# Keys transposed on VectorE and moved with the queries, under one written order for all engines

## The chip, the cores and the metric

The kernel runs on one core of a Trainium2 chip. The metric is the device time of one execution in microseconds, the median of the runs. A profiled execution gives the span from the first to the last instruction and a record of each instruction.

## The reference

Two blocks follow each other. A gated linear recurrence with a complex gate runs over 768 steps for 4 x 8 sequences of width 48, and its result is the input of a feed-forward block with 3072 tokens, 384 features and 2048 hidden units. All data are float32; the weights arrive as float64.

```python
mag = sqrt(a_re**2 + a_im**2)
a = (a_re + 1j*a_im) * minimum(mag, 0.999) / (mag + 1e-6)
for t in range(768):                       # per batch b of 4 and head h of 8
    S = a[t][:, None] * S + outer(k[t], v[t])
    y[t] = q[t] @ real(S)
x = y, heads side by side                   # (3072, 384)
h = x @ w_in                                # (3072, 2048)
g = h * erf(softplus(h))
out = g @ w_out                             # (3072, 384)
```

## The kernel before

`quotient_path` does the work; `product_path` is a general fallback behind a branch that tests the range of the data, and these inputs do not enter it. The tokens are cut into NU = 12 units of 256, each of C = 2 chunks of 128 tokens. Three units make one of the four sequences in time.

The recurrence is written as attention with decay. The gate's magnitude and angle are summed over time by matmuls against triangular matrices (`g_decay` or `g_total`, `g_angle`: tiles `sum`), and ScalarE makes exponentials (`pr`) and sines and cosines (`CS`) of the sums. VectorE multiplies q and k by them (`prep`: `qr`, `qt`, `kr`, `kt`), which gives rows of 96 numbers per head, the real and the imaginary half side by side. For the scores both must lie with the 96 on partitions. Scores are then masked (`A`), and `xT` adds A times v and the query times the carried state S (tiles `y`), 32 columns at a time in four column groups of TensorE. `state` makes the next S from k and v (tile `kv`).

How q and k come into columns is what the change touches:

- In unit 0, `cols` transposes q and k by TensorE (against `ident`, tile `tr`, L1009), and a copy brings them to `Q` and `kT` (L1018).
- From unit 1 on, q goes another way: `turn` lets VectorE transpose blocks of 32 x 32 (`X`, L1025), and 12 DMAs a chunk on SyncE's queue (SP) move the blocks to their partitions (`Q`, L1030). `Q` and `X` have one buffer each. k still goes through `cols`: 8 transposes on TensorE and two copies on ScalarE a chunk.

The feed-forward part works by units too: `ff_in` (tile `hps`, L1109, then a copy to `h`), `softplus` (four passes of ScalarE over 128 x 2048), `erf_times_h` (a Gelu on ScalarE and four passes of VectorE), and `ff_out_8` or `ff_out_7` (tiles `ops`, L1169 and L1207), the latter with seven products in place of eight by sums of blocks. The weights come as 64-bit words and are narrowed to float32 in 16 pieces by `narrow` (tiles `raw`, `word`, L790 to L806), and are read a second time (`again`) to be looked through. `w_in_sb` is laid out as 128 x 3 x 2048, so a piece of 256 hidden units is three runs in each partition.

The order of the work is set by a plan: each step has a due time in units (`WHEN`), the steps are sorted by it and issued in that order,

```python
    for _, f in sorted(plan, key=lambda e: e[0]):
        f()
```

and a scheduler then arranges the instructions of each engine. For the first steps, and for ScalarE where its function tables change, the order is kept as issued (`InOrder`, `in_order`). `warm` issues matmuls whose result is not read.

Of the kernel before, what the change touches and what calls it, by code (L numbers as in the profile page):

```python
# [35 lines left out]
def weave(*streams):  # L36
# [5 lines left out]
    for _, _, _, step in sorted(order, key=lambda e: e[:3]):  # L42
# [4 lines left out]
WHEN = {'a00': [0.2503, 0.7795, 0.1335, 0.1031, -0.5748, 0.1112, 0.3413, 0.3135, 0.2977, 0.4533],  # L47
 'a01': [0.4583, -0.1745, 0.4592, 0.4654, 0.4351, 0.5509, 0.5645, 0.5706, 0.5738, 0.6413],
 'n': [0.9645, 0.7895, 0.7814, 0.9723, 0.9993, 1.2454, 1.3547, 1.3732, 1.6259, 1.9835, 1.9666, 2.0634, 2.0911, 2.6653, 2.517],
 'g1': [0.7386, 0.7506, 0.7936, 0.8248, 0.8347, 0.8715, 0.878],  # L50
 'att': {1: [[0.9545, 1.3618], 1.0648], 2: [[1.7319, 2.0993], 0.8095], 3: [[3.0299, 3.594], 1.0991]},
 'gate': {2: [1.2001, 1.3019, 1.3116, 1.4094, 1.3878, 1.4777, 1.3631],
          3: [1.4851, 1.5487, 1.7904, 1.9989, 2.1384, 2.0754, 2.128],
          4: [2.4992, 2.6362, 2.8477, 3.2431, 3.3368, 3.699, 2.4826]},
 'hps': {0: [[0.7464, 0.847], [1.0328, 1.4318]],
         1: [[1.783, 2.003], [2.3859, 2.68]],
         2: [[2.8628, 3.209], [3.3359, 3.9229]],
         11: [[12.1478, 12.1509], [12.3502, 12.7439]]},
 'act': {0: [1.8595, 2.395],
         1: [3.3067, 3.698],  # L60
         2: [4.1613, 4.4383],
         3: [4.9661, 5.2089],
         4: [5.7479, 6.0159],
         10: [12.0452, 12.2596],
         11: [12.5676, 13.0911]},
 'ops': {0: [3.4509, 3.4886, 3.7821],
         1: [3.4648, 4.4529, 4.6258],
         2: [4.5583, 4.8264, 5.0683],
         3: [5.5746, 5.649, 6.1029],
         10: [11.9993, 12.5968, 12.9211],  # L70
         11: [13.0067, 13.2826, 13.5712]},
 'T': 5.3262,
 'gr': [-1.4884, -1.4376, -1.1567, -0.9311, -0.6027, -0.494, -1.1755],
 'st': [-0.0295, 0.1798, 0.1707, 0.2187, 0.2039, 0.2378, 0.3865],
 'lead': {0: -0.1195, (1, 0): -0.0719},
 'turn': [0.0319, 0.043],
 'lq': -0.6408,
 'hr': [1.1054, 1.4916, 1.607, 1.9359],
 'ar': [1.4604, 1.9924],
 'or': [2.1463, 2.6719, 3.1818],  # L80
 'c1': 0.4351,
 'er': 0.201,
 'ag': [5.3391, 6.7346, 7.1057, 8.2917, 8.8347, 10.8654, 10.6123],
 'n1': 2,
 'rest': 11.7803,
 'ok': 13.7659,
 'al': [[11.1278, 12.8576], [11.9156, 12.5677]],
 'c1g': [0.7517, 0.7897, 0.4817],
 'warm': 0.025}


WARM = (20, 0, 16, 2, 10, 6)

class InOrder:


    def __init__(self, tc, engine):
        self.tc, self.engine, self.on = tc, engine, False

    def __getattr__(self, name):  # L100
        emit = getattr(self.engine, name)
        if not self.on:
            return emit
        return lambda *args, **kw: self.tc.keep_in_program_order(emit(*args, **kw))
# [510 lines left out]

@with_exitstack
def quotient_path(
# [20 lines left out]
    vector, scalar = InOrder(tc, nc.vector), InOrder(tc, nc.scalar)  # L638
# [44 lines left out]
    cold = zp.tile([P, P], FP, tag="z", name="cold")  # L683
    vector.memset(cold, 0.0)
# [12 lines left out]
    w_in_sb = const.tile([P, KD, FF], FP, name="w_in_sb")  # L697
# [19 lines left out]
    order = mybir.DependencyInfo(mybir.DependencyClass.NoSync, mybir.DependencyReason.DATA)  # L717

    def act(func, **kw):
        sets = [nm for nm, fs in TABLES.items() if func in fs]  # L720
        if not sets:
            ins = scalar.activation(func=func, **kw)
            if T.get("kept"):
                in_order(ins)
            return
        if T.get("table") != sets[0]:
            T["table"] = sets[0]
            in_order(scalar.preload_act_table_set(sets[0]))  # L728
        in_order(scalar.activation(func=func, **kw))  # L729

    def in_order(ins):
        if "act" in T:
            tc.add_manual_dep(ins.ins, T["act"].ins.name, order, reason="table order")
        T["act"] = ins
# [5 lines left out]


    def load(pool, names, sources, u, engines, cc=(0, C)):
        for nm in names:
            if cc[0] == 0:
                T[nm, u] = pool.tile([P, C, H, D], FP, tag=nm, name=nm)
        for c in range(*cc):
            for nm, src, engine in zip(names, sources, engines):
                engine.dma_start(out=T[nm, u][:, c], in_=rows(src, u, c))

    def load_gates(u):  # L750
        if u < NU:
            load(lda, ("ar", "ai"), (a_re, a_im), u, (nc.sync, nc.sync if u > 0 else nc.scalar))

    def load_qkv(u, cc=(0, C)):
        if 0 <= u < NU:
            load(ldq, ("k", "q"), (k, q), u, (nc.sync, nc.sync), cc)
            t = T["v", u] = vbuf[u % 2]
            for c in range(*cc):
                for e in range(2):
                    src = rows(v, u, c).rearrange("t (h e) d -> e t h d", e=2)[e]  # L760
                    nc.sync.dma_start(out=side(t[:, c], e), in_=src)
# [6 lines left out]
    def narrow(i, dst, src, home):  # L768

        k_, n = dst.shape[1:]

        def seek(words, i):
            hi = words.bitcast(FP).rearrange("p (n w) -> p n w", w=2)[:, :, 1]
            vector.tensor_reduce(out=zeros[:, i:i + 1], in_=hi, axis=mybir.AxisListType.X, op=OP.min,  # L777
                                    apply_absolute_value=True)

        split = lambda t: t.rearrange("p (k n) -> p k n", k=k_)  # L780

        def get():
            T["raw", i] = home[0].tile([P, N], I64, tag=home[1], name="raw")
            nc.sync.dma_start(out=split(T["raw", i]), in_=src)

        def high():
            words = T["raw", i].bitcast(U32).rearrange("p (k n w) -> p k n w", k=k_, w=2)
            lo, hi = words[..., 0], words[..., 1]
            a = split(sp.tile([P, PARTS], U32, tag="S", name="word")[:, 0:N])
            ins = vector.tensor_scalar(out=a, in0=hi, scalar1=0x07FFFFFF, scalar2=3, op0=OP.bitwise_and,  # L790
                                       op1=OP.logical_shift_left)
            if "hold" in T:
                tc.add_manual_dep(ins.ins, T["hold"].ins.name, order, reason="place among others")
            vector.scalar_tensor_tensor(out=a, in0=hi, scalar=0xC0000000, in1=a, op0=OP.bitwise_and,
                                        op1=OP.bitwise_or)
            T["parts", i] = a, lo

        def low():
            _, lo = T["parts", i]
            ins = scalar.mul(out=lo, in_=lo, mul=2.0**-29)  # L800
            if i < 3:
                in_order(ins)

        def join():
            a, lo = T["parts", i]
            vector.tensor_tensor(out=dst.bitcast(U32), in0=a, in1=lo, op=OP.add)  # L806

        def use():
            high()
            low()  # L810
            join()

        def again():
            pool, tag = ((zp, "z"), (yp, "yy"))[i % 2]
            T["raw", i] = pool.tile([P, N], I64, tag=tag, name="again")
            nc.sync.dma_start(out=split(T["raw", i]), in_=src)

        def look():
            seek(T["raw", i], i)

        if i < 14:
            return get, use, again, look, high, low, join

        def again():
            for j, tag in enumerate(("ar", "ai")):
                T["raw", i, j] = lda.tile([P, n], I64, tag=tag, name="again")
                nc.sync.dma_start(out=T["raw", i, j], in_=src[:, j])

        def look():
            for j in range(2):  # L830
                seek(T["raw", i, j], 2 * i - 14 + j)

        return get, use, again, look, high, low, join

    def weights():

        none = lambda: None
        homes = [(rawp, "raw")] * 2 + [(hp, "h0")] * 2 + [(hp, "h1")] * 2 + [(rawp, "raw")] * 10
        steps = []
        for j in range(8):  # L840
            piece = (slice(None), slice(None), slice(j * 2 * P, (j + 1) * 2 * P))
            steps.append((w_in_sb[piece], w_in.rearrange("(i p) f -> p i f", p=P)[piece]))
# [16 lines left out]
    def sums_of_weights(r0, n):  # L859


        if r0 == 0:
            T["T1"], T["T2"] = [rawp.tile([P, 10, HD], FP, tag="raw", name=nm) for nm in ("T1", "T2")]
# [120 lines left out]
    def chunk(u, c):  # L984
# [17 lines left out]
        def cols(nm, g):  # L1002
            def f():
                if (nm, g) == ("q", 0):
                    columns()
# [440 lines left out]
```

## Time and profile before

| | |
|---|---|
| median of 3 runs | 716.7 us (714.72 to 717.21) |
| the profiled execution's own time | 716.54 us |
| its span | 714.8 us |
| TensorE busy | 685.7 us |
| VectorE busy | 575.5 us |
| ScalarE busy | 588.9 us |
| mean granted clock of TensorE | 0.987 |
| DMA packets on SP's queue | 166536, 61.88 MB |

In the profile PE is TensorE's matmuls, PEld its weight loads (which lie beside matmuls), DVE is VectorE, ACT ScalarE, SP SyncE, whose queue issues nearly all DMAs. Busy time is the union of an engine's instructions. In a row of a group, the two numbers after the bar are the busy time of the group in us and the mean of one instruction in ns; matmuls overlap, so their mean is longer than the distance from one to the next. An f32 matmul appears as two records, an f32 transpose as one. The last column is the idle time of the engine just before the group, and what ended it.

### The profile page before, as it was taken

The numbers are of one execution on the slowest core, as the hardware profiler recorded it, in microseconds if no ns is written. First come the engines' busy times: TensorE is split into PE (matmuls) and PEld (weight loads), VectorE is DVE, ScalarE is ACT, GpSimd is POOL, SyncE is SP. The second block draws the span as 40 slices with busy tenths as digits, with TensorE's granted clock in tenths as the row PEclk, the third lists the DMA queues.
The fourth block names the chain that finished last, engine by engine and source line by source line (L and its number), as shares of the span: only waits on it lengthen the run. The fifth ranks groups of instructions, "written<-read, shape, count | busy, mean of one in ns | idle before, by whom it ended". The sixth has DMA issues, their size and how long they took to land.

```text
span 714.8 us, 12640 instructions
## 1 busy us (share of the span) xinstructions
PE 685.7 (96%) x4872; PEld 584.1 (82%) x4872; DVE 575.5 (81%) x987; ACT 588.9 (82%) x763; POOL 1.1 (0%) x8
## 2 busy tenths in 40 slices
PE   9898898999999999999999999999999999999995
PEld 8777676776786767898998898898888898899984
DVE  6759889997686869999897989788998885977562
ACT  7777799999899978799997799798898864777660
POOL 0000000000000000000000000000000000000000
PEclk9889999999999999999999999999999999999998
DMA  9872866572222212434135433435225115000000
GB/s 205 234 177 54 185 155 154 142 121 48 64 52 66 45 45 43 135 69 90 23 81 152 123 64 82 123 68 164 36 56 134 24 39 183 24 1 11 12 24 28
DMA packets 168686, 63.18 MB, mean 88 GB/s; under 512 B 146836, under 2 KB 158376, under 8 KB 168616
## 3 DMA queue, kind: packets, MB, share of 16 engines
q1 hardware_dynamic: 166536, 61.88, 36.5%
q8 instruction: 40, 0.66, 0.4%
q10 hardware_dynamic: 2080, 0.39, 0.4%
q14 instruction: 30, 0.25, 0.1%
HBM read 48.82 MB, written 4.75 MB: 75 GB/s over the span
## 4 chain that ended last, share of the span: by engine, by line
PE 39%; ACT 30%; DVE 17%; DMA 7%; issue 3%; SPq 2%; DVEq 0%; ACTq 0%
PE hps L1109 14%; PE ops L1207 8%; ACT L728 7%; ACT yy L729 6%; ACT z L729 5%; PE ops L1169 4%; PE sc L1039 3%; PE y L1087 3%; DVE yy L1138 3%; DVE z L1137 3%; DVE e L1139 2%; ACT e L729 2%; DVE h L1140 2%; SPq L1030 2%; DMA again<-in_moe_w_out_dram 2%
## 5 line engine op out<-in xcount | busy, mean ns | idle before, releaser
L1109 PE MATMUL hps<-xT,w_in_sb 128*128 128x256 f32 x1152 | 270.5, 383 | 4.3 <-DVE w_in_sb L806 3.3
L1109 PEld LDWEIGHTS hps<-xT,w_in_sb 128*128 128x128 f32 x1152 | 215.0, 191 | 41.0 <-DVE w_in_sb L806 4.7
L728 ACT ACT_TABLE_LOAD x94 | 120.6, 1283 | 1.5
L1137 DVE TENSOR_TENSOR z<-z,yy 128x512 f32<-128x512 f32 x96 | 63.0, 684 | 32.3 <-ACT e L729 31.6
L729 ACT ACTIVATE e<-z 128x512 f32<-128x512 f32 x96 | 57.3, 627 | 30.8 <-DVE h L1140 30.4
L1111 ACT COPY h<-hps 128x512 f32<-128x512 f32 x96 | 55.0, 575 | 32.8 <-PE hps L1109 32.7
L1169 PE MATMUL ops<-w_out_sb,h 128*128 128x384 f32 x224 | 77.9, 490 | 0.6 <-DVE h L1140 0.5
L1207 PE MATMUL ops<-w_out_sb,h 128*128 128x192 f32 x384 | 71.7, 328 | 0.2 <-DVE o L1218 0.2
L1207 PEld LDWEIGHTS ops<-w_out_sb,h 128*128 128x128 f32 x384 | 63.9, 190 | 3.8 <-issue 1.0
L1138 DVE SCALAR_TENSOR_TENSOR yy<-z,yy 128x512 f32<-128x512 f32 x96 | 62.9, 682 | 0.4
L1139 DVE TENSOR_TENSOR e<-e,yy 128x512 f32<-128x512 f32 x96 | 62.9, 682 | 0.3
L1140 DVE SCALAR_TENSOR_TENSOR h<-e,h 128x512 f32<-128x512 f32 x96 | 63.0, 681 | 0.2
L1169 PEld LDWEIGHTS ops<-w_out_sb,h 128*128 128x128 f32 x224 | 41.4, 190 | 25.8 <-DVE o L1177 1.2
L1039 PE MATMUL sc<-Q,kT 96*128 96x128 f32 x384 | 50.7, 284 | 6.7 <-DMA Q<-X 2.6
L729 ACT ACTIVATE z<-h 128x2048 f32<-128x2048 f32 x24 | 45.9, 1914 | 13.1 <-DVE seen L777 10.1
L1039 PEld LDWEIGHTS sc<-Q,kT 96*128 96x128 f32 x384 | 48.0, 197 | 10.7 <-ACT kT L1018 4.4
L1207 PE MATMUL ops<-T,S 128*128 128x192 f32 x256 | 46.8, 327 | 0.1
L729 ACT ACTIVATE z<-z 128x2048 f32<-128x2048 f32 x24 | 45.9, 1911 | 0.3
L729 ACT ACTIVATE yy<-yy 128x2048 f32<-128x2048 f32 x24 | 45.9, 1913 | 0.3
L729 ACT ACTIVATE yy<-z 128x2048 f32<-128x2048 f32 x24 | 45.9, 1912 | 0.2
L1042 DVE TENSOR_TENSOR A<-sc,triu 128x512 f32<-128x512 f32 x48 | 32.5, 683 | 14.9 <-PE sc L1039 14.8
L1207 PEld LDWEIGHTS ops<-T,S 128*128 128x128 f32 x256 | 42.6, 190 | 1.8 <-DVE S L1221 0.7
(128 smaller groups left out, 996.2 us busy)
## 6 DMA issues: line engine op xcount, KB each, us to landing
Q<-X SPq DMA_DIRECT2D x264, 32.0 KB
raw<-in_moe_w_in_dram SPq DMA_DIRECT2D x8, 768.0 KB
raw<-in_moe_w_out_dram SPq DMA_DIRECT2D x8, 768.0 KB
again<-in_moe_w_in_dram SPq DMA_DIRECT2D x8, 768.0 KB
ar<-in_a_re_dram SPq DMA_DIRECT2D x24, 192.0 KB
k<-in_k_dram SPq DMA_DIRECT2D x24, 192.0 KB
q<-in_q_dram SPq DMA_DIRECT2D x24, 192.0 KB
v<-in_v_dram SPq DMA_DIRECT2D x48, 96.0 KB
```

The lines of the kernel that those rows point to most:

```text
L728: in_order(scalar.preload_act_table_set(sets[0]))
L729: in_order(scalar.activation(func=func, **kw))
L1039: nc.tensor.matmul(out=ps[:, j, :], lhsT=head("k", g * HG + j), rhs=head("q", g * HG + j), start=True, stop=True)
L1042: vector.tensor_tensor(out=A, in0=ps, in1=triu.unsqueeze(1).to_broadcast([P, HG, P]), op=OP.mult)
L1109: nc.tensor.matmul(out=ps[:, e, :], lhsT=w_in_sb[:, kd, f0:f0 + P], rhs=T["xT", u][:, kd, :], start=(kd == 0), stop=(kd == KD - 1))
L1111: scalar.copy(out=T["h", u, sl][:, i:i + 2, :], in_=ps)
L1137: vector.tensor_tensor(out=z, in0=z, in1=y, op=OP.mult)
L1138: vector.scalar_tensor_tensor(out=y, in0=z, scalar=-2.0, in1=y, op0=OP.add, op1=OP.mult)
L1139: vector.tensor_tensor(out=e, in0=e, in1=y, op=OP.mult)
L1140: vector.scalar_tensor_tensor(out=h, in0=e, scalar=1.0 / RT2, in1=h, op0=OP.add, op1=OP.mult)
L1169: nc.tensor.matmul(out=ps, lhsT=lhsT, rhs=w_out_sb[:, i, :], start=i == HALF, stop=i == KF - 1)
L1207: ins = nc.tensor.matmul(out=ps, lhsT=a(sl)[:, i], rhs=b(sl, i), start=sl == 0 and i == 0, stop=sl == NSL - 1 and i == HALF - 1)
```

## The change

1. From unit 1 on, keys go the way of the queries. `prep` lets VectorE transpose `kt` as well as `qt` into one tile `X` of twice the size, and `move` carries both at once: 12 DMAs a chunk as before, into one tile `KQ` of 16 heads (8 of k, 8 of q). Each head's 128 columns lie together in `KQ`, and a DMA fills 32 of them in each head. `X` and `KQ` have one buffer each. TensorE's transposes and the copies of `kT` remain in unit 0 alone.
2. Each step is a generator that stops where the engine changes, and one list, `ORDER`, names which step goes on next; a name appears once for each part of the step. The instructions of all engines stand in this order and no scheduler moves them. `WHEN`, `InOrder` and the manual dependencies are gone.
3. `w_in_sb` is laid out as 128 x 8 x 3 x 256, so that a piece is one run in each partition.
4. In `result` (before: `xT`) the products with A and with the state alternate as A, state, state, A instead of A, state, A, state. The warm-up matmuls read `ident`, and their number and places are in the list.

The diff, cut to its core:

```diff
-    w_in_sb = const.tile([P, KD, FF], FP, name="w_in_sb")
+    w_in_sb = const.tile([P, FF // (2 * P), KD, 2 * P], FP, name="w_in_sb")
...
-        def turn():
-            x = att1.tile([P, D2 // QUAD, H, QUAD], FP, tag="X", name="X")
-            src = st["q"].rearrange("p h u d -> p h (u d)").rearrange("p h (b d) -> p b h d", d=QUAD)
-            vector.transpose(out=x, in_=src)
-            columns()
-            for i in range(P // QUAD):
-                at = slice(i * QUAD, (i + 1) * QUAD)
-                for b in range(D2 // QUAD):
-                    nc.sync.dma_start(out=st["Q"][b * QUAD:(b + 1) * QUAD, i], in_=x[at, b])
...
+    def prep(nm, u, c):
...
+        if u > 0:
+            x = whole(att1, "X", (u, c), [P, D2 // QUAD, 2 * H, QUAD])
+            src = t.rearrange("p h u d -> p h (u d)").rearrange("p h (b d) -> p b h d", d=QUAD)
+            i = "kq".index(nm) * H
+            vector.transpose(out=x[:, :, i:i + H], in_=src)
+            yield
+
+    def columns(u, c):
+        return whole(att2, "KQ", (u, c), [P, 2 * H, P], bufs=1)
+
+    def move(u, c):
+        kq, x = columns(u, c), T["X", (u, c)]
+        for i in range(P // QUAD):
+            at = slice(i * QUAD, (i + 1) * QUAD)
+            for b in range(D2 // QUAD):
+                nc.sync.dma_start(out=kq[b * QUAD:(b + 1) * QUAD, :, at], in_=x[at, b])
+            yield
...
-    plan += [(WHEN["rest"], restore), (WHEN["ok"], check)]
-    for _, f in sorted(plan, key=lambda e: e[0]):
-        f()
+    with tc.manual_schedule():
+        for nm in ORDER.split():
+            if nm[0] == "u":
+                steps[nm] = warm(int(nm[1:].split("_")[0]))
+            next(steps[nm])
```

The list begins and goes on like this (`M` is a chunk's move, `A` scores and mask, `Y` the result, `K` and `Q` the preparation, `h`, `x`, `e`, `O` the feed-forward steps; the numbers are unit, chunk or slab, and part):

```python
ORDER = """
g0.0 u8_0 u2_40 u2_24 u4_38 u2_41 g0.0 u8_1 u2_39 u4_20 u2_25 u4_21 u2_34 g0.1 g0.1 t0.0 t0.0 o0.0 m0.0 m0.0
...
O2.14 e3.0.4 b4 h3.1.4 h3.1.4 h3.1.2 h3.1.2 x3.1 x3.1 x3.1 M5.0 M5.0 g7.0 M5.0 M5.0 a6.1 p6.0 p6.0 b0 S5.0 a6.1
```

## The prediction

> **What bounds the kernel now.** I read the first part of the page first (who is busy), then the groups by line (what the change touches), the waits of TensorE (PE), the windows by stage, and last a piece of the chain of waits.
>
> ```profile
> span 714.8 us, 12640 instructions
> PE 685.7 (96%) x4872; PEld 584.1 (82%) x4872; DVE 575.5 (81%) x987; ACT 588.9 (82%) x763; POOL 1.1 (0%) x8
> ```
>
> PE is busy 96% of the span; VectorE (DVE) and ScalarE (ACT) have a fifth to spare as a mean. The groups by line (count, then busy us and mean ns of one):
>
> ```profile
> L1009 PE MATMUL tr<-ident,kt 128*96 128x128 f32 x192 | 25.3, 273 | 2.6 <-DVE kt L995 2.3
> L1018 ACT COPY kT<-tr 96x512 f32<-96x512 f32 x46 | 25.3, 576 | 3.4 <-PE tr L1009 3.4
> L1025 DVE STREAM_TRANSPOSE X<-qt 128x768 f32<-128x768 f32 x22 | 21.3, 967 | 0.0
> ```
>
> The first two rows are what goes, the third is what comes a second time. Then who PE waited for (us in total, times, longest):
>
> ```profile
> PE hps L1109 <- DVE w_in_sb L806: 3.3, 3, 2.4
> PE sc L1039 <- DMA Q<-X: 2.6, 3, 1.0
> ...
> PE tr L1009 <- DVE kt L995: 2.3, 2, 2.0
> PE sc L1039 <- ACT kT L1018: 2.1, 3, 1.3
> ```
>
> All of PE's idle time is only 714.8 - 685.7 = 29.1 us, in many small pieces. By stage (windows; busy us of each engine, then the granted clock, the DMA engines' share and GB/s):
>
> ```profile
> 0.00:54.00 54.00, 49.72 (x359) 42.84 (x360) 35.55 (x72) 39.62 (x80) 1.08 (x8) 0.91 0.90 205
> 54.00:126.00 72.00, 63.77 (x516) 51.05 (x515) 63.73 (x101) 61.65 (x87) 0.00 (x0) 0.98 0.56 135
> 126.00:324.00 198.00, 195.70 (x1274) 151.75 (x1274) 165.24 (x276) 181.09 (x224) 0.00 (x0) 1.00 0.36 77
> 324.00:632.00 308.00, 301.29 (x2281) 271.12 (x2280) 261.48 (x449) 262.07 (x327) 0.00 (x0) 1.00 0.34 84
> ```
>
> From 126 to 632 us PE is the bound (98 to 99%), and from there to 702 us it is never idle. In 54 to 126 DVE is as full as PE (89%), ACT just behind; in 126 to 324 ACT is at 91%. Last the chain, from one result (y) to the next scores (sc):
>
> ```profile
> 606.85 2.59 PE hps L1109 x12
> 609.44 1.94 PE y L1087 x64
> ...
> 617.65 0.59 SPq L1030
> ...
> 618.29 1.83 DMA Q<-X
> ...
> 620.36 2.02 PE sc L1039 x16
> 622.39 1.30 PE ops L1207 x8
> ```
>
> It gives PE's paces: hps 2.59/12 = 0.216 us a record (an f32 matmul is two records, a transpose one), 192-wide ops 0.163, sc 0.112 within its group, y 0.030; in the same way 384-wide ops 0.323, kv 0.083, sums 0.323, tr 0.109 (in the timeline eight begin at 323.17 and the next group at 324.05). Every group's count times its pace is 657 us. So of 714.8 us, 58 are loss: up to the end of the y at 128.1 us 98.8 us of work are done (29 lost: start, half clock near 35 us), up to the y that ends at 634.2 it is 584 (21 more), then 0 until 707, and 7.8 for the last stores and the check.
>
> **The change part by part.**
>
> *K's transposes leave PE.* 22 chunks (all but the two of unit 0) x 8 = 176 of the 192: at the pace of 0.109 us 19.2 us, at the row's union (25.3/192 = 0.132) 23.2. Inside a row of matmuls the pace counts, so I take 19.2. This is on the bound.
>
> *ACT:* 44 copies of kT x 0.576 = 25.3 us go; in the new order of instructions ACT loads 3 tables more (100 for 97) x 1.283 (the mean of that row) = 3.8 come. Net -21.5, beside PE's work.
>
> *DVE:* 22 transposes more x 0.967 = 21.3 us (575.5 to 597). Beside PE where DVE has room; not in 54 to 126, where it is at 89%. Units 1 to 3 are prepared by about 150 us: 6 x 0.97 = 5.8 us fall there, and in the same stretch 6 x 8 x 0.109 = 5.2 us of PE's saving. I count 3 us of it as not realised.
>
> *The moves.* As many as before (12 a chunk, 264 on SP's queue), each 64 KB instead of 32, and the destination's runs fall from 1 KB to 32 elements of 4 bytes = 128 B: 512 packets for 32. Issue on SP is 0.59 us for a Q move, 0.5 to 0.6 for the loads of q, k and v with 512 to 1024 packets, so SP's issue costs the same; what the page does not show is the price of a 128 B packet. Bounds from the trace's windows:
>
> ```profile
> 315.00:318.00 3.00, 3.00 (x21) 3.00 (x20) 1.25 (x3) 2.97 (x6) 0.00 (x0) 1.00 0.16 39
> 324.00:327.00 3.00, 3.00 (x20) 2.74 (x19) 3.00 (x6) 2.99 (x5) 0.00 (x0) 1.00 1.31 225
> ```
>
> In the first only Q moves run: 0.16 x 16 engines x 3 us = 7.7 engine-us for 117 packets of 1 KB, 66 ns each; by bytes 128 B would be 8 ns, the lower end. In the second the loads of k, q and v run, in runs of 192 B: 62.9 engine-us for 675 KB, 18 ns a packet. 192 B is the nearest row, so I take 18: 512 x 18 / 16 = 0.58 us a move, still under SP's 0.63 from issue to issue. The Trainium skill speaks against the change here: "DMA: Bandwidth & Descriptors", section Specifications, wants 512 B and more for line rate, and says that below it the engine reads, modifies and writes. Were that a doubling of 18 ns, a move would be 1.15 us and the set of 12 would last 14 us instead of 7.6. The 192 B row already contains whatever short runs cost (225 GB/s, no less than the 205 of the first 54 us, where weights come in long runs too), so I hold to 0.58 and keep 1.15 as the upper end.
>
> *Who waits for the moves.* K and Q of a chunk lie in one buffer, as Q alone did. So the loop is: y of the chunk before ends, 12 issues, landing, scores: in the chain above 611.38 to 620.36 = 9.0 us; with K inside I add the last move's extra 0.4 and take 9.5 to 10. In the new order PE has, between these two points, work of 9.7 us at the least (chunk 1.1), 10.4 twice, else 11 to 27 (by the paces above). (The first chunk of a sequence has no state to read; there I count from its scores.) Before it was 7.3 to 8.7 in three places, which is the wait of 2.6 us. So the moves cost 0 to 1 us and that wait may shrink. On DVE the transposes of the next chunk now wait until this chunk's moves have been read; they stand mostly behind this chunk's A, which is later anyway.
>
> *Weights by pieces.* Pieces of w_in_sb no longer interleave, so a matmul need not follow the writing of a piece that it doesn't read: at most 3.3 us (the wait on w_in_sb); the two waits around kT and kt are another 4.4, partly in unit 0, which keeps its transposes. I take -4 for all.
>
> *One list.* PE's groups are laid out in longer runs, 46 warm-up matmuls for 54 and none after the first scores. This can shift any of the 50 us lost before 634 us. One piece has a name: near 31 to 42 us the clock is at one half, after a wait of 2.03 us, and 10 us of matmuls cost some 5 extra. The skill ("TensorE: Matmul & The Clock Gate", Part 1) has the clock fall to half after an idle window of about 3.4 us; by it a start with fewer warm-ups could pay this once more (+5), by the trace it was paid with the warm-ups too. I take 0, and ±10 for the list.
>
> Sum: 714.8 - 19.2 + 3 + 1 - 4 = 695.6 of span, against the profiled execution's own 716.54 (1.7 around the span); the median of the runs is 716.7, 0.2 above. 695.6 + 1.9 = 697.5; I say 697.
>
> **The rivals.** *DVE becomes the bound of the first half.* Adding DVE's rows along both orders: up to the masks A of chunk 6.0, 287 us of DVE work stand in the new order beside 286 of PE; before, 276 beside 300. DVE has lost its lead of 24 us, and idled 59 us by then (324 - 264.5). If it idles 45 in the new order, PE is 10 us later than I count, and the next stage (85% DVE) gives little back: 697 + 9 = 706. For it: 89% in 54 to 126; against: half its idle time was waiting for PE.
>
> *The list packs better.* If the start loses 22 instead of 29 and the middle 13 instead of 21: 697 - 15 = 682. Against: three engines at 90% leave little to pack.
>
> *The moves become the loop (slower).* If a 128 B packet costs over 30 ns (a move 0.96 us, y to scores 14 us), the gaps of PE's work are too short in over half of the chunks; summed over the 22 the waits are about 21 us at 14 us, which eats the gain, and 45 at 16 us (the doubled price): 697 + 45 - 14 (half of the waits moves into other idle time later) = 728. For it: the rule above; against: the 18 ns of the 192 B loads, and the DMA engines at about 0.35 after 126 us, where 264 x (512 x 18 - 32 x 66) ns = 1.9 ms of 11.4 ms of engine time add only 0.16.
>
> That the transposes do not go is excluded: the order of PE's instructions has 16 of K's left.
>
> **How the numbers follow.** Main case (690 to 703) 0.50; DVE as bound (to 712) 0.20; better packing (about 682) 0.14; moves slower 0.12; within 0.3% (2.2 us, about what a measurement of this kernel can tell) 0.04. Faster by over 0.3% is 0.50 + 0.20 + 0.14 = 0.84. The range leaves out the slow case and the best of the good: 682 to 715.
>
> **What would show it.** Right: tr x16 for kt, no ACT COPY kT but six KQ copies, 44 stream transposes of about 0.97 us, moves at 0.6 us on SP, PE's busy time near 666, waits of sc on DMA KQ<-X under 5 us. DVE rival: waits of PE on A and h above 10 us before 320 us. Moves rival: y to sc at 14 us and more, and sc <- DMA KQ<-X over 20 us. I am wrong if PE's busy time falls by 19 us and the span does not.

## The result, and the profile after

The changed kernel takes 687.7 us (median of 4 runs, 687.09 to 689.06) against 716.96 us for the kernel before on the same chip (4 runs, 714.72 to 720.71): a ratio of 0.959, with a 95% interval of 0.955 to 0.963. The prediction was 697, with a range of 682 to 715.

First the head of the page and, under it, the summary of the chain that ended last (share of the span by engine):

```profile
span 685.5 us, 12236 instructions
...
PE 655.0 (96%) x4680; PEld 560.1 (82%) x4680; DVE 619.1 (90%) x1008; ACT 578.0 (84%) x722; POOL 1.1 (0%) x8
...
DVE 32%; ACT 32%; PE 26%; issue 4%; DMA 3%; SPq 2%; DVEq 0%; POOL 0%; ACTq 0%; POOLq 0%
```

The span is 29.3 us shorter. PE's busy time fell by 30.7 us (685.7 to 655.0) and its idle time hardly moved (29.1 to 30.5). Read alone, that says "PE was the bound, work was taken from it, the time followed". The last line says something else. In the kernel before the same line was

```profile
PE 39%; ACT 30%; DVE 17%; DMA 7%; issue 3%; SPq 2%; DVEq 0%; ACTq 0%
```

so PE held the largest part of that chain; now DVE and ACT hold a third each and PE a quarter. The experiments follow that second reading.

The groups that the change touches (count, busy us and mean ns of one, then the idle time before):

```profile
L1004 PE MATMUL tr<-ident,kt 128*96 128x128 f32 x16 | 2.9, 310 | 0.5 <-DVE kt L980 0.5
L1008 ACT COPY KQ<-tr 96x512 f32<-96x512 f32 x6 | 3.2, 573 | 0.3 <-PE tr L1004 0.3
L986 DVE STREAM_TRANSPOSE X<-qt 128x768 f32<-128x768 f32 x22 | 21.2, 965 | 0.1
L986 DVE STREAM_TRANSPOSE X<-kt 128x768 f32<-128x768 f32 x22 | 21.2, 964 | 0.0
```

The 176 transposes of K are gone from PE, and VectorE has 22 more of 0.964 us. PE's waits that answer to those shown of before (us in total, times, longest):

```profile
PE sc L1017 <- ACT KQ L1008: 3.0, 2, 1.8
PE y L1066 <- DVE A L1021: 2.1, 2, 1.3
...
PE sc L1017 <- DMA KQ<-X: 1.9, 2, 1.2
PE hps L1079 <- ACT h L1082: 1.9, 5, 0.6
```

The wait on `w_in_sb` (3.3 us) is no longer there, and the one on the moves is 1.9 us for 2.6. By stage (busy us and count of PE, its weight loads, DVE, ACT and POOL, then clock, DMA share and GB/s):

```profile
0.00:54.00 54.00, 41.37 (x329) 33.40 (x330) 42.21 (x81) 44.91 (x84) 1.09 (x8) 0.94 0.94 212
54.00:126.00 72.00, 69.53 (x516) 56.49 (x515) 68.91 (x104) 65.82 (x89) 0.00 (x0) 1.00 0.83 165
126.00:324.00 198.00, 193.37 (x1322) 152.93 (x1321) 189.62 (x303) 176.18 (x210) 0.00 (x0) 1.00 0.48 89
324.00:600.00 276.00, 272.83 (x2055) 247.77 (x2054) 261.45 (x421) 245.12 (x290) 0.00 (x0) 1.00 0.49 103
```

DVE is at 96% from 54 to 324 us (before: 89% and 83%) and at 95% up to 600; PE is at 97 to 99%. There is little room left on either; the next section tests what that means.

### The profile page after: what moved, and what is told of

It is laid out like the page before. It is cut to its first block, busy times and chain, and to the rows that moved or that the text cites. A ratio compares the mean times of both kernels' runs of the same rounds, so it can differ in the third digit from the quotient of the medians.

```text
span 685.5 us, 12236 instructions
## 1 busy us (share of the span) xinstructions
PE 655.0 (96%) x4680; PEld 560.1 (82%) x4680; DVE 619.1 (90%) x1008; ACT 578.0 (84%) x722; POOL 1.1 (0%) x8
## 4 chain that ended last, share of the span: by engine, by line
DVE 32%; ACT 32%; PE 26%; issue 4%; DMA 3%; SPq 2%; DVEq 0%; POOL 0%; ACTq 0%; POOLq 0%
PE hps L1079 10%; ACT L754 7%; ACT yy L755 7%; ACT z L755 7%; DVE yy L1108 4%; DVE e L1109 4%; DVE h L1110 4%; DVE z L1107 4%; PE Z L1179 2%; ACT e L755 2%; ACT CS L755 2%; PE Y L1179 2%; PE X L1179 2%; PE sc L1017 2%; PE unread L1235 2%
## 5 line engine op out<-in xcount | busy, mean ns | idle before, releaser
L1079 PE MATMUL hps<-xT,w_in_sb 128*128 128x256 f32 x1152 | 263.0, 381 | 3.1 <-ACT h L1082 1.9
L1107 DVE TENSOR_TENSOR z<-z,yy 128x512 f32<-128x512 f32 x96 | 65.7, 685 | 13.3 <-ACT e L755 13.2
L1108 DVE SCALAR_TENSOR_TENSOR yy<-z,yy 128x512 f32<-128x512 f32 x96 | 66.4, 692 | 3.3
L1109 DVE TENSOR_TENSOR e<-e,yy 128x512 f32<-128x512 f32 x96 | 66.4, 692 | 3.3
L1144 PEld LDWEIGHTS ops<-w_out_sb,h 128*128 128x128 f32 x224 | 42.1, 190 | 26.5 <-issue 0.4
L1017 PEld LDWEIGHTS sc<-KQ 96*128 96x128 f32 x384 | 47.6, 194 | 10.7 <-ACT KQ L1008 3.6
L1017 PE MATMUL sc<-KQ 96*128 96x128 f32 x384 | 50.2, 281 | 5.9 <-ACT KQ L1008 3.0
L1066 PE MATMUL y<-A,v 128*32 128x128 f32 x768 | 34.9, 282 | 2.8 <-DVE A L1021 2.1
L1028 PEld LDWEIGHTS kv<-v,kt 128*96 128x96 f32 x320 | 29.9, 165 | 3.9 <-ACT pr L755 1.2
L1028 PE MATMUL kv<-v,kt 128*96 128x48 f32 x320 | 29.9, 246 | 0.8 <-ACT pr L755 0.6
L1066 PEld LDWEIGHTS y<-A,v 128*32 128x32 f32 x768 | 21.5, 112 | 10.7 <-DVE A L1021 4.1
```

The costliest lines, as they stand in the source:

```text
L1017: nc.tensor.matmul(out=ps[:, j, :], lhsT=head("k", g * HG + j, u, c), rhs=head("q", g * HG + j, u, c), start=True, stop=True)
L1028: nc.tensor.matmul(out=kv[0:D2, j, :], lhsT=T["kt", u, c][:, j].rearrange("p u d -> p (u d)"), rhs=side(T["v", u][:, c, j // 2], j % 2), s ...
L1066: nc.tensor.matmul(out=ps[b * QUAD:(b + 1) * QUAD, i, :], lhsT=lhsT, rhs=rhs, start=start, stop=stop)
L1079: nc.tensor.matmul(out=ps[:, e, :], lhsT=w_in_sb[:, (sl * SLAB + i) // 2, kd, e * P:(e + 1) * P], rhs=T["xT", u][:, kd, :], start=(kd == 0 ...
L1107: vector.tensor_tensor(out=z, in0=z, in1=y, op=OP.mult)
L1108: vector.scalar_tensor_tensor(out=y, in0=z, scalar=-2.0, in1=y, op0=OP.add, op1=OP.mult)
```

## The experiments

All ratios are to the kernel before on the same chip, with their 95% intervals; "cost" is the median against 687.7 us. An interval of 0.4% to either side makes each cost uncertain by about 4 us; the runs were made on three chips, and costs worked out from the ratios would differ from these by up to 3 us.

| kernel | us | ratio | cost |
|---|---|---|---|
| transposes_on_pe_unread (PE +19) | 696.6 | 0.972 (0.968 to 0.976) | +8.9 |
| q_transposed_twice (DVE +21.2) | 701.8 | 0.981 (0.978 to 0.985) | +14.1 |
| tables_22_more (ACT +28.2) | 709.2 | 0.990 (0.986 to 0.994) | +21.5 |
| weights_interleaved | 703.8 | 0.982 (0.978 to 0.986) | +16.1 |
| y_products_alternate | 688.8 | 0.961 (0.957 to 0.965) | +1.1 |
| warm_in_the_gaps | 686.8 | 0.959 (0.955 to 0.962) | -0.9 |
| two_steps_on_pool | 695.8 | 0.970 (0.967 to 0.973) | +8.1 |
| moves_in_24 | 850.4 | 1.190 (1.182 to 1.197) | +163 |
| keys_on_pe_in_list | 757.5 | 1.058 (1.055 to 1.061) | +70 |
| keys_on_pe_later_copies | 743.6 | 1.036 (1.032 to 1.039) | +56 |
| keys_moved_no_list (on the kernel before) | 825.0 | 1.152 (1.149 to 1.156) | |
| pieces_alone (on the kernel before) | 719.7 | 1.004 (1.002 to 1.007) | |

### A dose for each engine

Three kernels add to one engine what the change moved there or away, and change nothing else.

TensorE: the 176 transposes, of the identity, into the score tile that the scores then overwrite.

```diff
+        for j in range(HG if u > 0 else 0):
+            nc.tensor.transpose(out=ps[0:D2, j, :], in_=ident[:, 0:D2], identity=ident)
         for j in range(HG):
             nc.tensor.matmul(out=ps[:, j, :], lhsT=head("k", g * HG + j, u, c), rhs=head("q", g * HG + j, u, c),
```

> The changed kernel with 8 transposes a chunk more on TensorE in units 1 to 11 (176 in all, of the identity, into the score tile ahead of its matmuls; nobody reads them, nothing waits for them, no copies): the dose of TensorE work that the change took away, given back by itself. Theory (TensorE's work counts at its pace, 0.109 us each): +19, a little less where they fill a wait: 703 to 708. Rival (VectorE, 95% busy between 54 and 600 us and hurt by two thirds of an added dose, is the bound now, and TensorE's saving is worth half or less): 690 to 698.

Measured +8.9 us, and not 19: the rival's number. PE's busy time rose by 18.4 us (673.4), its idle time fell from 30.5 to 22.1. Some half of the dose fell into PE's idle pieces.

VectorE: each query's transpose twice.

```diff
-            vector.transpose(out=x[:, :, i:i + H], in_=src)
+            for _ in range(2 if nm == "q" else 1):
+                vector.transpose(out=x[:, :, i:i + H], in_=src)
```

> The changed kernel with each query's VectorE transpose done twice (the same result written again): 22 x 0.965 = 21.2 us more on VectorE, nothing else changed. Theory (TensorE is the bound, VectorE's extra work lies beside it but for the first 126 us, where it is full): 6 of the 22 fall there, +3 to +6 us, and the rest +0 to +3: 691 to 697. Rival (VectorE, busy 90% now, sets the end with TensorE): two thirds and more of it show, 702 to 709.

Measured +14.1 us: the rival's number again, two thirds of the dose. The windows of this kernel, from 126 us:

```profile
126.00:324.00 198.00, 189.58 (x1276) 149.18 (x1275) 192.30 (x302) 174.59 (x206) 0.00 (x0) 1.00 0.46 86
324.00:600.00 276.00, 267.59 (x1981) 240.04 (x1981) 265.85 (x425) 236.39 (x285) 0.00 (x0) 1.00 0.50 104
```

DVE, third in the row of busy times, is now at 97 and 96%, and PE has 3.8 and 5.2 us less to do in the same stretches than in the changed kernel: DVE makes PE wait, in many places and nowhere for long (the longest wait of PE on DVE or ACT is 1.8 us).

ScalarE: 22 table loads of 1.283 us.

```diff
             vector.transpose(out=x[:, :, i:i + H], in_=src)
+            if nm == "k" and T.get("table"):
+                scalar.preload_act_table_set(T["table"])
```

> The changed kernel with 22 loads more of the table that ScalarE already has, one beside each chunk's key transpose: 22 x 1.283 = 28.2 us more on ScalarE, nothing else changed; about what the 44 copies of keys cost it before (25.3). Theory of the prediction (ScalarE's saving lies beside TensorE's work): 688 to 692. Rival (the three engines are coupled so tightly that ScalarE's time shows as VectorE's does, two thirds of it): 700 to 708.

Measured +21.5 us of 28.2, or 0.76 for each us, and the theory of the prediction had allowed 4. PE now waits for `xT` 6.8 us and for `h` 6.5, and DVE for `e` 31.2 us where it was 13.2. So the time of ScalarE, busy only 84% of the span, shows no less than that of the others.

With 4 us of uncertainty the shares that show are 0.26 to 0.67 for TensorE, 0.48 to 0.86 for VectorE and 0.62 to 0.90 for ScalarE. They overlap, so the order of the three is not shown; that all three count is, since each cost is clear of zero, and so is that TensorE's dose does not count in full. The chain of the page follows the dose each time: PE's part went from 26 to 64% in the first kernel,

```profile
PE 64%; DVE 14%; ACT 11%; SPq 4%; DMA 4%; issue 2%; POOL 0%; DVEq 0%; POOLq 0%
```

DVE's from 32 to 51% in the second and ACT's from 32 to 42% in the third. A part of the chain says which engine was last in one run, and not what an added us on it costs.

### The weights' layout

```diff
-    w_in_sb = const.tile([P, FF // (2 * P), KD, 2 * P], FP, name="w_in_sb")
+    w_in_sb = const.tile([P, KD, FF], FP, name="w_in_sb")
```

(with the indices of `piece` and `ff_in` to match)

> The changed kernel with w_in_sb laid out as before (128 x 3 x 2048), so that the pieces interleave again. Theory (a matmul then waits for the writing of pieces that it does not read, 3.3 us before): 689 to 692. Rival (with the order written in a list the pieces are written well ahead of the matmuls, and the layout is worth nothing): 687 to 688.5.

Measured +16.1 us, nearly four times the theory's upper end. In the timeline of PE (start, duration, idle before it in brackets), first this kernel, then the changed one:

```profile
60.11 4.64 PE L1079 MATMUL hps<-xT,w_in_sb 128*128 128x256 f32 x10 [6.01 <-DVE w_in_sb L818]
...
72.88 9.29 PE L1079 MATMUL hps<-xT,w_in_sb 128*128 128x256 f32 x29 [6.20 <-DVE w_in_sb L818]
```

```profile
54.72 5.13 PE L1079 MATMUL hps<-xT,w_in_sb 128*128 128x256 f32 x23
60.40 5.45 PE L1079 MATMUL hps<-xT,w_in_sb 128*128 128x256 f32 x24 [0.55 <-ACT h L1082]
```

The matmuls of the first feed-forward groups stand in the list ahead of the narrowing of later pieces. Interleaved, a group waits for pieces that it does not read: twice 6 us. And each wait costs a second time: after 6.01 us of idleness 10 records take 4.64 us, or 0.46 each, where the changed kernel needs 5.13/23 = 0.22. The window shows why (PEclk is the number after POOL):

```profile
61.00:73.00 12.00, 5.80 (x28) 4.53 (x27) 6.76 (x9) 4.91 (x7) 0.00 (x0) 0.64 0.59 121
```

The same edit on the kernel before, the other way round:

> The kernel before with w_in_sb by pieces as the only change (due times and scheduler as they are). Theory (the pieces are worth much only together with the list, which places the first feed-forward groups ahead of the narrowing of later pieces; before, the wait was 3.3 us in three places): 712 to 716. Rival (the pieces are worth the 16 us that they are worth in the changed kernel, whatever the order): 699 to 703.

Measured 719.7 against 716.73 (12 and 17 runs): no gain, 0.4% slower if anything. PE's wait on `w_in_sb` was 2.5 us in its profile for 3.3. The layout is worth 16 us in this written order and shows no gain under the plan that was there before.

### The moves

```diff
             for b in range(D2 // QUAD):
-                nc.sync.dma_start(out=kq[b * QUAD:(b + 1) * QUAD, :, at], in_=x[at, b])
+                for s in (slice(0, QUAD // 2), slice(QUAD // 2, QUAD)):
+                    nc.sync.dma_start(out=kq[b * QUAD:(b + 1) * QUAD, :, at][:, :, s], in_=x[at, b][:, :, s])
```

> The changed kernel with each move cut into two of 64 B runs: 24 DMAs a chunk for 12, the same bytes, twice the packets and twice the issues on SyncE's queue (12 x 0.63 = 7.5 us more a chunk, and 165 us more on the queue). Theory of the prediction (the loop from y to the next scores grows from 9.5 to about 17 us, and TensorE's work between the two is 10 to 27 us): waits of scores on the moves of 30 to 50 us, 710 to 735. Rival (the moves start early enough and other work can run ahead, so the loop has slack): under +8, 688 to 696.

Measured +163 us; both theories were far too low. The waits, and two score groups from the timeline:

```profile
PE sc L1018 <- DMA KQ<-X: 91.7, 17, 8.2
PE sc L1018 <- DMA wrow<-pr: 25.7, 4, 8.0
```

```profile
425.84 3.75 PE L1018 MATMUL sc<-KQ 96*128 96x128 f32 x16 [7.09 <-DMA KQ<-X]
...
463.67 2.02 PE L1018 MATMUL sc<-KQ 96*128 96x128 f32 x16 [2.57 <-DMA y<-F]
```

The waits of scores are 120 us in 22 places (the two rows and one of 2.6). In sum PE is idle for 111 us more than in the changed kernel. The other 53 us are busy time: PE is busy 707.7 us with the same 4680 records for which it needed 655.0, and its granted clock is 0.90 as a mean for 0.99. After 7.09 us of idleness the 16 records of `sc` take 3.75 us, after 2.57 us they take 2.02. The granted clock behind the first:

```profile
426.00:430.00 4.00, 4.00 (x18) 4.00 (x19) 1.06 (x2) 0.00 (x0) 0.00 (x0) 0.50 1.04 334
```

The loop was also longer than the 17 us that I had expected: in most places 18 to 25 us from the end of y to the scores. Before the second group above, y ends at 439.4 us and the last issue at 462.0. Of these 22.6 us the 24 issues take 16.5; 2.9 pass before the first, and in the other 3.3 transfers of other chunks (`wrow`, `w`, `y`) stand between them on the same queue. The changed kernel, on SP's queue at a like place (start and time that the issues took):

```profile
542.32 1.98 SPq L997 DMA_DIRECT2D KQ<-X  x3
544.34 0.62 SPq L1134 DMA_DIRECT2D out_dram<-out  x1
545.00 1.06 SPq L782 DMA_DIRECT2D v<-in_v_dram  x2
546.10 5.97 SPq L997 DMA_DIRECT2D KQ<-X  x9
```

Here 12 moves and 3 others take 9.8 us (y ended at 541.8, the scores began at 556.0 without a wait). It is the count of issues on that queue, 0.63 us each (the median, in both kernels), that sets the loop. The packets do not: while the 24 moves were issued the DMA engines were busy at 0.37 (the number before the last).

```profile
444.00:456.00 12.00, 12.00 (x74) 11.28 (x74) 11.55 (x20) 10.23 (x14) 0.00 (x0) 1.00 0.37 35
```

The line of the queue (packets, MB, share of 16 engines), of before and of after:

```profile
q1 hardware_dynamic: 166536, 61.88, 36.5%
```

```profile
q1 hardware_dynamic: 293256, 70.53, 50.4%
```

that is 4174 and 5528 engine-us (share x 16 x span). If all other transfers cost what they did, and before's 264 x 32 packets 66 ns each as in the prediction, the 264 x 512 packets of 128 B cost (5528 - 4174 + 558)/135168 = 14 ns each, and a move 0.45 us, less than its issue. The records of the single packets in the two traces agree: as a mean 13.6 ns for the packets of 128 B, and 58 ns for those of 1 KB. So the short ones cost nearly twice as much for each byte, and still do not set the loop.

### Keys back on TensorE, and keys moved without the list

Both undo or take half of the change, and both are much slower than before. First the list with K's transposes and copies put back by hand, here at chunk 1.0 (the first two `kT` are the transposes, the other two the copies; in the second version the copies stand later):

```diff
-        if u > 0:
-            x = whole(att1, "X", (u, c), [P, D2 // QUAD, 2 * H, QUAD])
+        if u > 0 and nm == "q":
+            x = whole(att1, "X", (u, c), [P, D2 // QUAD, H, QUAD])
...
-Y0.1 n7 v2.1
+Y0.1 kT1.0.0 kT1.0.1 kT1.0.0 kT1.0.1 n7 v2.1
```

> The changed kernel (687.7 us) with one part undone: keys of units 1 to 11 are transposed by TensorE again and copied by ScalarE, at the places in the list that are nearest to where KQ is free; the list, the weights by pieces and the order of y's products stay; the moves carry q alone. Theory (TensorE is the bound, each transpose costs its pace): 176 x 0.109 = 19.2 us come back, and up to 5 more where the copies are late: 705 to 712. Rival (the list is what made the kernel faster; with 44 table and copy places free, the transposes fit into TensorE's idle time): 688 to 694. Rival (VectorE is the bound in the first half, and is relieved of 22 transposes = 21.2 us): 695 to 702.

> As keys_on_pe_in_list (757.5 us, where ScalarE stood 44 us at the copies into KQ with nothing else to do, because I had put them just behind the y of the chunk before), with the transposes a little earlier in the list and the copies two thirds of the way from y to the chunk's own scores, all on ScalarE. Theory from the doses measured on the changed kernel (TensorE +8.9 for 19.2 us, ScalarE 0.76 for each us x 25.3 = +19, VectorE -0.67 x 21.2 = -14): 702, with 698 to 708. Rival of the prediction (TensorE alone is the bound): 705 to 708, with TensorE's waits as in the changed kernel. Rival (a list made for another order of copies cannot take them in by hand): 715 and more, with ScalarE waiting for tr over 20 us.

The first version does not do all that its expectation says: `turn` still gave the copies of each unit's first chunk to VectorE, as in unit 0. VectorE made 22 of the 44 (0.679 us each) and was relieved of some 6 us and not of 21, so the last rival of that run was not tested. In the second version ScalarE makes all 44.

Measured 757.5, which fits neither the theory nor a rival, and 743.6, in the range of the last rival. In the first, ScalarE stands at the copies:

```profile
ACT KQ L1010 <- PE tr L1006: 36.4, 6, 13.8
ACT KQ L1010 <- DMA v<-in_v_dram: 8.0, 1, 8.0
```

In the second those waits are gone, against that rival's own sign, and PE has 16.7 us on `kt` and 11.0 on `KQ` in their place. The granted clock is 0.963 as a mean in both, for 0.992. What these two runs show is the price of a badly placed step in a fixed order; they do not tell what K on TensorE would cost in a list made for it. That stays open.

Then the kernel before, with K moved and everything else as it was:

```diff
+            for j, nm in enumerate("kq"):
+                src = st[nm].rearrange("p h u d -> p h (u d)").rearrange("p h (b d) -> p b h d", d=QUAD)
+                vector.transpose(out=x[:, :, j * H:(j + 1) * H], in_=src)
...
-            return [prep("q", 0), turn, prep("k", 1), cols("k", 0), cols("k", 1), state,
+            both = lambda: (prep("q", 0)(), prep("k", 1)())
+            return [both, turn, none, none, none, state,
```

> The kernel before (717.0 us) with one part of the change alone: keys are transposed by VectorE and moved with the queries in the same 12 DMAs; the plan with its due times, the scheduler and the weights' layout stay. Theory (each part gives what it takes from TensorE, whoever orders it): 717.0 - 19 = 698, with 695 to 703 as the range; then the list and the rest are worth about 10 us. Rival (the due times were fitted to transposes on TensorE, and only the list makes the moves early enough): 706 to 716, and waits of scores on the moves above 10 us. Rival (the list adds nothing): 686 to 690.

Measured 825.0 us. The transposes left PE as planned, but the waits of the profile are of another kind than the rival named:

```profile
PE y L1086 <- DVE A L1041: 27.3, 12, 5.9
PE ops L1170 <- DVE h L1141: 25.3, 6, 11.0
...
PE sc L1038 <- DMA KQ<-X: 4.5, 1, 4.5
```

By these rows it is mostly VectorE that is late, and hardly the moves; the granted clock is 0.92 as a mean for 0.987. I prepared k at q's due time, earlier than before; which part of the 108 us is due to that, and which to due times that no longer fit, was not separated.

### Two attempts to do better, and the order of y's products

```diff
-        vector.tensor_tensor(out=a, in0=T[nm, u][:, c], op=OP.mult,
+        (nc.gpsimd if nm == "q" and u > 0 else vector).tensor_tensor(out=a, in0=T[nm, u][:, c], op=OP.mult,
...
-        vector.tensor_tensor(out=S[:, sl], in0=A21, in1=A22, op=OP.add)
+        nc.gpsimd.tensor_tensor(out=S[:, sl], in0=A21, in1=A22, op=OP.add)
```

> The changed kernel with two VectorE steps given to GpSimd, which is idle: the products q x pr of units 1 to 11 (22 x 0.546 = 12.0 us) and the sums S of units 3 to 10 (16 x 0.68 = 10.9 us). Theory (VectorE is a bound together with TensorE and ScalarE; two thirds of an added dose showed): 22.9 us less on VectorE give 5 to 15 us: 673 to 683. Rival (GpSimd is slower at them and stands in VectorE's way at the memory, so that queries or VectorE's other rows come later): 690 and more, with VectorE's 128 x 512 rows longer than 0.69 us.

Measured +8.1 us. The product takes 1.397 us on GpSimd for 0.546 on VectorE, and VectorE waits 5.0 us in the next step for the sums. VectorE's four passes of `erf_times_h` are hardly longer (0.692 to 0.699 us for 0.685 to 0.692), but `qt` is 1.013 for 0.949, the subtraction that follows the sum in the program is 0.979 for 0.692, and VectorE's busy time fell by only 2.5 us of 22.9. So both halves of the rival have signs; how much each step costs was not separated.

```diff
-r0.0 a0.0 a0.0
+r0.0 u6_90 a0.0 a0.0
...
-qT0.0.1 qT0.0.0 kT0.0.1
+u6_91 qT0.0.1 qT0.0.0 kT0.0.1
...
-p0.1 n1
+u4_92 p0.1 n1
...
-qT0.0.0 A0.0.0 A0.0.0
+qT0.0.0 u6_93 A0.0.0 A0.0.0
```

> The changed kernel with 22 warm-up matmuls more in four idle pieces of TensorE between 14 and 30 us (6, 6, 4, 6), each before a group that waits for another engine. Theory (the half clock from 27 to 36 us is TensorE's answer to these idle pieces; but VectorE is full from 27 us on and sets the pace there): the clock stays at 1.0 until 54 us, and the time falls by 0 to 3 us: 685 to 688. Rival (the warm-ups stand in the way of the short groups that ScalarE and VectorE wait for): 689 to 693. Rival (the half clock is paid in full): 682 to 684.

Measured -0.9 us, within the uncertainty. The half clock did not go, it came later:

```profile
30.00:33.00 3.00, 1.51 (x36) 1.05 (x35) 2.97 (x6) 2.97 (x5) 0.00 (x0) 1.00 1.17 204
...
39.00:42.00 3.00, 3.00 (x9) 1.48 (x8) 2.97 (x6) 2.38 (x6) 0.00 (x0) 0.50 0.40 66
```

In both rows DVE (the busy time after PE's two) is full, in the first ACT too. That agrees with the theory that they set the pace of the start.

```diff
-                    todo += both[::-1] if (len(steps[b]) + len(todo)) % 4 else both
+                    todo += both
```

> The changed kernel with the products of y in the order A, state, A, state as before. Theory (the order of the products does not change TensorE's pace): 687 to 689. Rival (two products after one another that share an operand's place run faster): 2 to 5 us slower, and the groups of y in the chain longer than 1.94 us.

Measured +1.1 us, within the uncertainty; y at 72.18 us takes 1.97 us in this kernel and, at 69.77, 1.95 in the changed one. The order of the products is worth nothing that can be seen.

## Why the prediction was right, and where its steps were not

The sum was 695.6 us of span against 685.5 measured, and the sign and the main cut were right. By the paces of the prediction's own ledger PE's work fell from 657 to 636 us, 19.2 for the transposes and 1.7 for fewer warm-ups. The losses fell too: from 29 to 25 us up to the y near 128 us, from 21 to 16 up to the one before the end, and the tail of 7.8 stayed. The prediction had put both at no change after its terms; these 9 us and the warm-ups are its miss. PE's busy time was to be near 666 us and was 655.0: its idle time did not fall, so the losses that fell lay inside busy time, where PE works at less than its pace.

- *K's transposes, -19.2 "on the bound".* The count (16 left), the copies (6 left) and the paces were right. That all of it counts was not: the same dose, added to the changed kernel, costs 8.9 (5 to 13).
- *ACT, -21.5 "beside PE's work".* This is the step that failed most. A dose of ScalarE shows at 0.76, so 21.5 us are worth about 16. The dose is of the changed kernel, and of table loads in other places than the copies had; that the copies cost as much in the kernel before is argued. There was a warning: ACT held 30% of the chain of before, next to PE's 39.
- *DVE, +21.3, of which 3 not realised.* Mis-sized: a dose shows at two thirds, so about 14. The sign that I had named for the DVE rival (waits of PE on A and h above 10 us before 320) never came, 2.1 and 1.9 us in the whole span, and VectorE is a bound all the same. DVE's busy time went to 619.1 and not to 597; the reason is below.
- *Weights by pieces, with the waits on kT and kt: -4.* Mis-sized. In the list the layout alone is worth 16, and nothing without the list. The waiting time of the old trace could not show it, because the new order reaches those matmuls earlier.
- *The list, 0 within 10.* No run has the list alone, so what it is worth by itself is not shown. The rival that packs better gave 682; the result lies between it and the main case.
- *The moves, +1.* Right: waits of 1.9 us, and 0.627 us per issue for the 0.6 that I gave. The packet was 14 ns for 18, and the doubling to 36 ns, kept as the upper end, is not there. The 12 issues of a chunk took 8.0 to 11.5 us, where I had given the whole loop 9.5 to 10, and 14 in one place where other transfers stand among them. The slower rival named packets, and those are cheap. But its mechanism, a loop longer than TensorE's other work, is real and dear: with 24 issues, loops of 18 to 25 us cost 163 us.
- *The half clock.* Paid once more, for 0 in the sum, but shorter. By the windows the clock stood at 0.50 for about 7 us (up to 36 us) in the changed kernel. In the kernel before it was about 10 us (31 to 42) and 3.4 more after a wait on `w_in_sb` at 62 us, and this second piece is gone. Half of the difference, some 3 us, is an estimate of its part in the 9.

Put together from the doses, -8.9 - 16 + 14 - 16 = -27 beside the measured -29. That agreement is a check of size and no proof: the doses were added to the fixed order of the changed kernel, the list itself stands at nothing in the sum, and the two keys-on-TensorE runs show that such prices do not simply add. But it suggests why 697 was near. By these prices the prediction gave PE's part 10 us too much and VectorE's cost 11 too little, and left out 16 of ScalarE's and 12 of the layout's; these errors nearly cancel. That the number lay within 10 us is in part luck. How the 29 us divide between the keys and the list stays open.

## What to carry to other kernels

When three in-order engines are each at 84 to 96% in one fixed order, "PE is 96% busy" does not make PE the only price: give each engine a small dose of extra work and read how much of it shows (here 0.47, 0.67 and 0.76 for PE, DVE and ACT, each to within 0.2), before costing a shift of work between them. Ask of a layout not how long the old order waited for it, but what the new order will ask of it. And count the issues on a DMA queue inside a loop before its packets, because a long wait (here 6 to 8 us) is paid again in TensorE's clock.

## What the runs showed of the hardware

*A VectorE instruction that needs the result of the one before it starts later.* In the changed kernel the four passes of a step stand behind one another:

```profile
401.66 0.68 DVE L1107 TENSOR_TENSOR z<-z,yy 128x512 f32<-128x512 f32 x1
402.38 0.69 DVE L1108 SCALAR_TENSOR_TENSOR yy<-z,yy 128x512 f32<-128x512 f32 x1
403.10 0.69 DVE L1109 TENSOR_TENSOR e<-e,yy 128x512 f32<-128x512 f32 x1
403.83 0.69 DVE L1110 SCALAR_TENSOR_TENSOR h<-e,h 128x512 f32<-128x512 f32 x1
404.44 0.68 DVE L1107 TENSOR_TENSOR z<-z,yy 128x512 f32<-128x512 f32 x1
```

Each of the first three is followed after 0.72 or 0.73 us by one that reads its result, the fourth after 0.61 by one that does not. It is so at 284 of the 288 such places of the changed kernel (0.72 to 0.73 us). Before, if the passes are paired in their order, the scheduler had put other instructions between at all but 24 places, and at those 24 the distance is 0.71 to 0.73 as well. In the lines below one stands between, and the start of the last less that of the first is 0.87 us for two instructions:

```profile
415.54 0.68 DVE L1137 TENSOR_TENSOR z<-z,yy 128x512 f32<-128x512 f32 x1
416.14 0.35 DVE L1218 SCALAR_TENSOR_TENSOR o<-ops,o 128x192 f32<-128x192 f32 x1
416.41 0.68 DVE L1138 SCALAR_TENSOR_TENSOR yy<-z,yy 128x512 f32<-128x512 f32 x1
```

Here is one of the four passes, before and after:

```profile
L1139 DVE TENSOR_TENSOR e<-e,yy 128x512 f32<-128x512 f32 x96 | 62.9, 682 | 0.3
```

```profile
L1109 DVE TENSOR_TENSOR e<-e,yy 128x512 f32<-128x512 f32 x96 | 66.4, 692 | 3.3
```

Over the four groups the busy time rose from 251.8 to 265.0 us and the gaps before the last three from 0.9 to 9.9, so the list lost some 22 us of VectorE here: as much as K's transposes cost it. An estimate: two steps woven together would save up to 3 x 96 x 0.11 = 32 us of VectorE, of which a dose of two thirds makes about 20 us. It was not tried.

*The clock fell after short waits too.* After single waits of 6 and 7 us it was at one half. The Trainium skill ("TensorE: Matmul & The Clock Gate", Part 1) has it fall after an idle window of about 3.4 us, and these two agree. But the length of the last wait does not decide it here. After 2.57 us the clock was at 1.00, while in the kernel before it was at one half after a wait of 2.03 us near 30 us and after one of 2.43 us, from 59.7 to 62.2 us (the clock is the third number from the end):

```profile
60.00:63.00 3.00, 0.83 (x2) 0.74 (x3) 3.00 (x7) 2.97 (x4) 0.00 (x0) 0.83 0.21 55
63.00:66.00 3.00, 3.00 (x10) 2.38 (x9) 3.00 (x5) 2.56 (x5) 0.00 (x0) 0.60 0.43 90
```

At the start of the changed kernel no wait before 30 us is above 1.9 us, and the clock still fell to 0.50:

```profile
27.00:30.00 3.00, 1.15 (x7) 0.96 (x7) 3.00 (x6) 2.95 (x8) 0.00 (x0) 0.88 0.90 283
30.00:33.00 3.00, 2.22 (x26) 1.85 (x29) 2.31 (x5) 2.97 (x5) 0.00 (x0) 0.50 1.04 189
```

There PE had been busy for 8.4 of the 15 us before, and idle in small pieces for the rest. What rule joins these cases no run here shows.
